# A linear-attention layer and a gated MLP in one kernel: the written order of the first part set anew

## The chip, the cores and the metric

One core of a Trainium2 chip runs the whole program. The time is the device time of one execution in microseconds (us); lower is better.

## The reference

Four sequences of 768 tokens with 8 heads of 48 channels go through a recurrent attention, and the 3072 resulting tokens of 384 channels through a gated MLP with 1536 hidden channels. All is in float32.

```python
# attention, for each batch and head, over t = 0 .. 767
cur   = outer(u * k[t], v[t])
y[t]  = r[t] @ (state + cur)
state = w[:, None] * state + outer(k[t], v[t])

# MLP on x = y, tokens by channels
gate = 1 / (1 + exp(-(x @ w_gate)))
out  = (gate * (x @ w_val)) @ w_out
```

## The kernel before, in words

**Attention.** The sequence is cut into 12 chunks of 64 steps, and the heads into two groups of four. `GROUPS` numbers the 24 pairs of chunk and head group: groups 0 and 1 are chunk 0, groups 2 and 3 are chunk 1, and so on. For a group, two input tiles come in: `chan` (queries and keys with channels on the partitions, step `L`, line 104) and `toks` (keys and values with tokens on the partitions, step `X`, line 109); each has three buffers. Of them are made, by powers of `w` in tables, scaled queries (`R`, line 309), keys (`k`, 320), keys with the bonus `u` (`A`, 296, which must read the keys before `k` writes over them), and token keys (`T`, 324). TensorE forms the scores (`Z`, line 392, 32 small matmuls, two instructions each of matmul and weight load), VectorE keeps the wanted half of them (`K`, 400), TensorE applies them to the values (`I`, 354; from chunk 1 on it adds the part from the state first, with a drain of TensorE between), and forms the outer products for the next state (`O`, 354). The result goes to the MLP's input as a rounded high part (`h`, 493, ScalarE) and a low part (`l`, 497, VectorE); the state is decayed (`d`, 447) and added to or, in chunk 0, copied (`s` on VectorE, `sa` on ScalarE, 468). Six or so small transfers fill spare rows of that input (`F`, line 501).

**MLP.** The MLP runs over tiles of 512 tokens (two chunks). The 1536 hidden channels are 12 weight blocks `f`. A product of float32 quality is made of three products of high and low parts. For a block, `u` and `v` (line 531) are nine matmuls each, gate and value; `g` (544, ScalarE), `m` (548, VectorE), `H` (553, ScalarE) and `q` or `qv` (557, GpSimd or VectorE) make the hidden values, and `D` (573) adds their product with the third weight matrix into three accumulators. The first tile takes blocks 0 and 1 in two halves of 256 columns, `a` (chunk 0) and `b` (chunk 1), because chunk 1 isn't there yet.

**Weights.** Each block is loaded once (`W`, line 242, 1152 KB; block 0 in two halves) and turned into high and low parts that stay: `c` (249, ScalarE), `j` (256, VectorE), `w` (264, ScalarE), and `o` or `ov` (267, GpSimd or VectorE). `c0`, `j0`, `w0`, `o0` with an index are the halves of block 0.

**The order.** No scheduler chooses the order: `manual_schedule` takes the instructions of all engines as they are written. The string `START` is the order of the first part. Each word is one step, and the word's place sets the place of its instructions in the queue of its engine. An engine runs its own queue in order and waits, by semaphores, for what others must have made. `N.5` is five idle matmuls on a spare tile (line 641), whose result nobody reads. After the string, a loop in the code runs the remaining tiles.

```python
    for step in START.split():
        name, _, arg = step.partition(".")
        if name == "D":
            finish(block(arg))
        elif name in moe_steps:
            moe_steps[name](moe_of(block(arg)), block(arg)[2])
        else:
            steps[name](*([int(arg)] if arg else []))
```

Matmul results of attention and of `u` and `v` share three PSUM banks (`ring`); a step that needs a bank waits for the readers of what stood there.

Of the kernel before, what the change touches and what calls it, by code (L numbers as in the profile page):

```python
# [40 lines left out]


START = """
ta L.0 tov.0 tc tb W.0 ts.0 L.1 ts.1 X.0 tz W.1 tk L.2 X.1 to.1 ti.1 X.2 ti.0 A.0 R.0 W.2 k.0 c0.0
tp tr Z.0 tt A.1 K.0 c0.1 tn k.1 I.0 Rv.1 j0.1 h.0 l.0 Tv.0 Z.1 c.1 j0.0 O.0 A.2 j.1 w0.0 sa.0 N.5
T.2 K.1 F.0 w.1 W.3 Rv.2 I.1 T.1 N.4 k.2 L.3 o0v.0 h.1 L.4 Z.2 w0.1 W.4 O.1 X.3 l.1 o0.1 s.1 u.0a
g.0a K.2 v.0a o.1 m.0a c.2 I.2 O.2 R.3 d.2 j.2 u.1a A.3 N.3 H.0a g.1a k.3 h.2 q.0a s.2 v.1a w.2 l.2
m.1a Z.3 T.3 A.4 H.1a N.4 R.4 K.3 c.3 k.4 I.3 O.3 F.2 L.5 W.8 o.2 D.0a X.4 h.3 L.6 Z.4 W.5 l.3 d.3
W.6 L.7 s.3 X.5 u.0b X.6 g.0b j.3 v.0b c.4 w.3 u.2 j.4 qv.1a m.0b H.0b g.2 v.2 q.0b K.4 w.4 Rv.5
u.1b T.4 A.5 v.1b g.1b m.1b D.0b k.5 H.1b I.4 ov.3 O.4 m.2 A.6 R.6 q.1b Z.5 k.6 L.8 d.4 D.1a W.7 h.4  # L50
o.4 s.4 H.2 D.1b K.5 c.6 l.4 Tv.5 u.3 c.5 g.3 j.6 v.3 j.5 qv.2 I.5 h.5 Z.6 l.5 R.7 L.9 A.7 m.3 X.8
d.5 D.2 ub K.6 H.3 O.5 k.7 s.5 w.5 q.3 u.4 c.8 T.6 ov.5 c.7 g.4 v.4 j.7 w.6 m.4 u.5 ov.6 g.5 v.5 I.6
Y.8 R.8 Z.7 W.9 d.6 O.6 W.10 X.7 w.7 W.11 H.4 s.6 X.9 D.3 j.8 h.6 qv.4 w.8 l.6 D.4 m.5 H.5 F.6 ov.7
qv.5 u.6 c.9 g.6 K.7 v.6 ov.8 m.6 Tv.7 H.6 u.7 qv.6 g.7 k.8 v.7 j.9 m.7 w.9 D.5 o.9 u.8 g.8 H.7 v.8
q.7 c.10 D.6 j.10 m.8 I.7 H.8 Z.8 O.7 d.7 R.9 h.7 w.10 s.7 D.7 b.8 ov.10 u.9 l.7 qv.8 g.9 c.11 v.9
F.7 Y.9 j.11 m.9 D.8 w.11 ov.11 u.10 g.10 H.9 qv.9 v.10 m.10 H.10 u.11 qv.10 g.11 t.8 i.8 v.11 K.8
k.9 m.11 D.9 H.11 t.9 D.10 q.11 b.9 T.9 i.9 T.8
"""


# [869 lines left out]
```

## Time and profile before

| | |
|---|---|
| time, median of 3 runs | 528.82 us (526.42 to 529.17) |
| the profiled execution | 528.38 us, its span 526.6 us |
| TensorE busy | 509.7 us (97%) |
| VectorE, ScalarE, GpSimd busy | 202.6, 186.1, 187.2 us (38, 35, 36%) |
| data moved by DMA | 47.84 MB, mean 91 GB/s |
| mean granted clock of TensorE | 0.995 |

The span goes from the first to the last instruction of the profiled execution; its own time has 1.8 us more around it. PE is TensorE's matmuls, PEld its weight loads, which overlap them; DVE is VectorE, ACT ScalarE, POOL GpSimd, SP the engine that issues the transfers. The granted clock is a share of 2.4 GHz: 0.50 is 1.2 GHz. "issue" as the cause of a wait means that the profile shows nothing that the engine waited for. No clock is on record before 16.46 us, and the table shows 1.00 there.

### The profile page before, as it was taken

The page shows a single profiled execution, that of the slowest core. Times are in us where ns is not written, and L with a number is a line of the kernel's source. Part 1 is how long each engine was busy: PE and PEld are TensorE (multiplying, and loading weights), DVE is VectorE, ACT ScalarE, POOL GpSimd, SP SyncE. Part 2 cuts the span into 40 slices and gives each one's busy share as a digit, 9 for nine tenths or more (in the row PEclk, how much of TensorE's full clock was granted, in tenths as well). Part 3 has the DMA queues.
Part 4 walks back from the last instruction along what each step waited for, and adds up shares of the span by engine and source line. Part 5 has one row for each costly group of instructions (what it writes and reads, how often), then busy time and mean ns, then how long its engine had stood idle before and what let it go on. Part 6 is the DMA issues. An engine that isn't in the chain of part 4 may idle for free.

```text
span 526.6 us, 11976 instructions
## 1 busy us (share of the span) xinstructions
PE 509.7 (97%) x5220; PEld 421.4 (80%) x5220; DVE 202.6 (38%) x345; ACT 186.1 (35%) x395; POOL 187.2 (36%) x158
## 2 busy tenths in 40 slices
PE   3899999999999999999999999999999999999995
PEld 3689788888888788888888888888888888888884
DVE  7877865545242243242341432431442211111112
ACT  5587864534223134233133332331431221311211
POOL 4454402214545252453452452552352111111120
PEclk9899999999999999999999999999999999999999
DMA  8949654123213030420230420312400000100001
GB/s 318 368 144 421 262 191 167 34 75 96 76 64 88 10 107 4 145 88 19 78 98 12 148 87 1 97 36 72 147 17 2 11 7 14 61 0 1 0 2 65
DMA packets 15579, 47.84 MB, mean 91 GB/s; under 512 B 2368, under 2 KB 4928, under 8 KB 14112
## 3 DMA queue, kind: packets, MB, share of 16 engines
q1 hardware_dynamic: 15376, 46.74, 25.5%
q8 instruction: 43, 0.70, 0.6%
q10 hardware_dynamic: 144, 0.26, 0.1%
...
## 4 chain that ended last, share of the span: by engine, by line
PE 95%; DVE 2%; DMA 1%; issue 1%; ACT 0%; SPq 0%; DVEq 0%; ACTq 0%
PE ring L531 56%; PE acc L573 29%; PE ring L354 7%; PE sc L392 3%; DMA chan<-in_ch 1%; DVE score L400 1%; DVE wf L256 0%; PE acc L641 0%; DVE chan L320 0%; ACT dec L296 0%; DVE sg L586 0%; DVE dec L309 0%; DVE xt L497 0%; DVE toks L324 0%; PE acc L354 0%
## 5 line engine op out<-in xcount | busy, mean ns | idle before, releaser
L531 PE MATMUL ring<-xt,wx 128*128 128x512 f32 (+1 forms) x1332 | 306.5, 384 | 0.0
L531 PEld LDWEIGHTS ring<-xt,wx 128*128 128x128 f32 x1332 | 245.2, 188 | 49.8 <-ACT sg L544 0.3
L557 POOL TENSOR_TENSOR h<-sg,h 128x512 fp32r<-128x512 f32 (+1 forms) x65 | 87.1, 1340 | 252.4 <-ACT h L553 252.4
L573 PE MATMUL acc<-h,wx 128*128 128x512 f32 (+1 forms) x666 | 161.3, 387 | 0.0
L573 PEld LDWEIGHTS acc<-h,wx 128*128 128x128 f32 x666 | 121.2, 188 | 25.0 <-DVE h L557 0.2
L548 DVE TENSOR_TENSOR sg<-ring,sg 128x512 f32<-128x512 f32 (+1 forms) x74 | 50.0, 676 | 235.0 <-PE ring L531 233.5
L544 ACT ACTIVATE sg<-ring 128x512 f32<-128x512 f32 (+1 forms) x74 | 43.2, 584 | 156.3 <-PE ring L531 156.3
L553 ACT CAST h<-sg 128x512 fp32r<-128x512 f32 (+1 forms) x74 | 45.0, 609 | 144.1 <-DVE sg L548 137.8
L309 POOL TENSOR_TENSOR dec<-chan,tabk 128x512 f32<-128x512 f32 x21 | 27.7, 1319 | 14.3 <-PE ring L354 14.0
L497 DVE TENSOR_TENSOR xt<-ring,xt 112x256 fp32r<-112x256 f32 (+1 forms) x52 | 19.9, 418 | 32.6 <-ACT xt L493 32.6
L324 POOL TENSOR_TENSOR toks<-toks,tabn 128x384 f32<-128x384 f32 x19 | 23.7, 1253 | 12.5 <-ACT wx L264 9.5
L330 POOL TENSOR_TENSOR dec<-dec,toks 128x384 f32<-128x384 f32 x16 | 16.3, 1017 | 26.9 <-DMA dec<-in_rt 26.7
L320 DVE TENSOR_TENSOR chan<-chan,tabk 128x512 f32<-128x512 f32 x24 | 24.8, 1034 | 0.6 <-ACT dec L296 0.6
L392 PE MATMUL sc<-dec,chan 48*64 48x64 f32 x768 | 17.2, 231 | 7.7 <-DVE chan L320 7.6
L400 DVE COPY_PREDICATED score<-masks,sc 128x512 f32<-128x512 int32 x32 | 23.9, 748 | 1.9 <-PE sc L392 1.1
L447 ACT ACTIVATE state<-state,pw 112x96 f32<-112x96 f32 x80 | 23.4, 362 | 1.8 <-PE ring L354 1.8
L392 PEld LDWEIGHTS sc<-dec,chan 48*64 48x64 f32 x768 | 14.8, 145 | 8.9 <-POOL dec L309 7.6
L466 DVE TENSOR_TENSOR state<-state,ring 48x192 f32<-48x192 f32 (+1 forms) x52 | 17.9, 350 | 8.1 <-PE ring L354 4.3
L256 DVE SCALAR_TENSOR_TENSOR wf<-wr,top 128x1152 int32<-128x1152 int32 (+1 forms) x13 | 16.8, 1304 | 9.5 <-ACT top L249 6.0
L354 PE MATMUL ring<-score,toks 64*48 64x64 f32 (+1 forms) x768 | 16.6, 223 | 3.7 <-issue 2.3
L493 ACT CAST xt<-ring 112x256 fp32r<-112x256 f32 (+1 forms) x52 | 16.7, 363 | 6.6 <-PE ring L354 6.4
L267 POOL TENSOR_TENSOR wx<-wf,wx 128x1152 fp32r<-128x1152 f32 (+1 forms) x5 | 12.5, 2507 | 18.3 <-ACT wx L264 18.3
...
## 6 DMA issues: line engine op xcount, KB each, us to landing
...
```

The costliest lines, as they stand in the source:

```text
L309: eng.tensor_tensor(v4(t[:, 0]), v4(chan[n][:, 0]), bc2(table_of(n)[:, :, ::-1]), ALU.mult)
L320: eng.tensor_tensor(v4(k), v4(k), bc2(table_of(n)), ALU.mult)
L324: eng.tensor_tensor(v4(k), v4(k), bc2(tabn[:, 4 * g : 4 * g + 4]), ALU.mult)
L354: nc.tensor.matmul(to[bank][64 * half : 64 * half + m, cs], lhsT, rhs, start=first, stop=stop, skip_group_check=True,)
L392: nc.tensor.matmul(sc[64 * gm : 64 * gm + 64, be, o : o + C], kk[row, cs : cs + C], rr[row, cs : cs + C], start=True, stop=True,)
L400: nc.vector.copy_predicated(t.rearrange("q (b m i) -> q b m i", b=2, m=4), masks[:, m].bitcast(I32).unsqueeze(1).unsqueeze(1).broadcast_to ...
L531: nc.tensor.matmul(o[:, self.cols], w[a][:, g * DM + kt * P : g * DM + (kt + 1) * P], self.x[:, kt, b, self.cols], start=(k == 0), stop=(k ...
L544: nc.scalar.activation(sg[:, c], self.pair[f][0][:, c], AF.Sigmoid, scale=UP)
L548: nc.vector.tensor_tensor(sg[:, c], self.pair.pop(f)[1][:, c], sg[:, c], ALU.mult)
L553: nc.scalar.copy(out=h[:, 0, c], in_=sg[:, c])
L557: eng.tensor_tensor(h[:, 1, c], self.sg.pop(f)[:, c], h[:, 0, c], ALU.subtract)
L573: nc.tensor.matmul(self.acc[d][:, self.cols], w[a][:, 2 * DM + d * P : 2 * DM + (d + 1) * P], h[:, b, self.cols], start=(f == 0 and k == 0 ...
```

## The change

Only the string `START` differs. The same steps are written in another order, some on another engine: five of the sixteen idle matmuls go (`N.5 N.4 N.3 N.4` becomes `N.5 N.4 N.1 N.1`), the first `to` (clearing a tile) goes from VectorE to GpSimd, `tr` becomes `trA` (VectorE to ScalarE), `sa.0` and `s.1` become `s.0` and `sa.1`, and some `R`, `T`, `o` and `q` change between GpSimd and VectorE. From `m.8 I.7 H.8` on, the two strings are the same again.

```diff
--- before.py
+++ after.py
@@ -41,20 +41,20 @@
 
 
 START = """
-ta L.0 tov.0 tc tb W.0 ts.0 L.1 ts.1 X.0 tz W.1 tk L.2 X.1 to.1 ti.1 X.2 ti.0 A.0 R.0 W.2 k.0 c0.0
-tp tr Z.0 tt A.1 K.0 c0.1 tn k.1 I.0 Rv.1 j0.1 h.0 l.0 Tv.0 Z.1 c.1 j0.0 O.0 A.2 j.1 w0.0 sa.0 N.5
-T.2 K.1 F.0 w.1 W.3 Rv.2 I.1 T.1 N.4 k.2 L.3 o0v.0 h.1 L.4 Z.2 w0.1 W.4 O.1 X.3 l.1 o0.1 s.1 u.0a
-g.0a K.2 v.0a o.1 m.0a c.2 I.2 O.2 R.3 d.2 j.2 u.1a A.3 N.3 H.0a g.1a k.3 h.2 q.0a s.2 v.1a w.2 l.2
-m.1a Z.3 T.3 A.4 H.1a N.4 R.4 K.3 c.3 k.4 I.3 O.3 F.2 L.5 W.8 o.2 D.0a X.4 h.3 L.6 Z.4 W.5 l.3 d.3
-W.6 L.7 s.3 X.5 u.0b X.6 g.0b j.3 v.0b c.4 w.3 u.2 j.4 qv.1a m.0b H.0b g.2 v.2 q.0b K.4 w.4 Rv.5
-u.1b T.4 A.5 v.1b g.1b m.1b D.0b k.5 H.1b I.4 ov.3 O.4 m.2 A.6 R.6 q.1b Z.5 k.6 L.8 d.4 D.1a W.7 h.4
-o.4 s.4 H.2 D.1b K.5 c.6 l.4 Tv.5 u.3 c.5 g.3 j.6 v.3 j.5 qv.2 I.5 h.5 Z.6 l.5 R.7 L.9 A.7 m.3 X.8
-d.5 D.2 ub K.6 H.3 O.5 k.7 s.5 w.5 q.3 u.4 c.8 T.6 ov.5 c.7 g.4 v.4 j.7 w.6 m.4 u.5 ov.6 g.5 v.5 I.6
-Y.8 R.8 Z.7 W.9 d.6 O.6 W.10 X.7 w.7 W.11 H.4 s.6 X.9 D.3 j.8 h.6 qv.4 w.8 l.6 D.4 m.5 H.5 F.6 ov.7
-qv.5 u.6 c.9 g.6 K.7 v.6 ov.8 m.6 Tv.7 H.6 u.7 qv.6 g.7 k.8 v.7 j.9 m.7 w.9 D.5 o.9 u.8 g.8 H.7 v.8
-q.7 c.10 D.6 j.10 m.8 I.7 H.8 Z.8 O.7 d.7 R.9 h.7 w.10 s.7 D.7 b.8 ov.10 u.9 l.7 qv.8 g.9 c.11 v.9
-F.7 Y.9 j.11 m.9 D.8 w.11 ov.11 u.10 g.10 H.9 qv.9 v.10 m.10 H.10 u.11 qv.10 g.11 t.8 i.8 v.11 K.8
-k.9 m.11 D.9 H.11 t.9 D.10 q.11 b.9 T.9 i.9 T.8
+ta tk L.0 to.0 tz X.1 tc A.0 ti.1 tb tp k.0 X.0 ti.0 to.1 L.1 R.0 trA W.0 Z.0 tt ts.0 c0.0 Rv.1 A.1
+tn L.2 K.0 k.1 I.0 h.0 ts.1 W.1 j0.0 l.0 w0.0 c0.1 R.2 Tv.0 L.3 A.2 X.2 Z.1 O.0 K.1 c.1 j0.1 N.5 s.0
+I.1 N.4 w0.1 T.1 o0.0 L.4 h.1 k.2 Z.2 j.1 O.1 l.1 K.2 R.3 F.0 I.2 Tv.2 W.2 u.0a o0.1 X.3 w.1 o.1 T.3
+A.3 k.3 d.2 O.2 N.1 X.5 g.0a T.5 h.2 A.4 v.0a N.1 W.3 sa.1 s.2 l.2 Z.3 F.2 c.2 u.1a m.0a K.3 k.4
+H.0a q.0a g.1a j.2 L.5 I.3 h.3 W.5 v.1a l.3 d.3 m.1a D.0a R.4 Z.4 O.3 u.0b s.3 c.3 W.4 u.1b w.2 v.0b
+g.0b ov.2 H.1a j.3 w.3 A.5 q.1a u.2 m.0b H.0b g.2 qv.0b v.2 g.1b W.6 c.5 m.2 j.5 D.0b o.3 u.3 L.6
+K.4 H.2 c.4 v.1b X.4 q.2 v.3 X.7 g.3 D.1a j.4 m.1b L.8 Rv.5 c.6 k.5 Tv.4 I.4 W.7 Z.5 O.4 w.5 m.3
+Tv.7 d.4 A.6 X.6 h.4 ov.5 R.6 w.4 k.6 s.4 K.5 ov.4 D.2 u.5 H.3 W.8 W.11 H.1b l.4 q.3 j.6 g.5 T.6 D.3
+qv.1b u.4 g.4 v.5 D.1b w.6 v.4 c.8 L.7 m.5 ub c.7 m.4 H.4 qv.4 W.10 o.6 j.8 u.6 I.5 d.5 Z.6 O.5 h.5
+g.6 A.7 D.4 j.7 s.5 K.6 l.5 H.5 v.6 R.7 I.6 w.7 W.9 o.7 q.5 k.7 c.9 Z.7 O.6 X.8 d.6 m.6 w.8 j.9 o.8
+u.7 h.6 c.10 H.6 D.5 g.7 l.6 s.6 v.7 u.8 v.8 qv.6 m.7 D.6 F.6 Y.8 w.9 L.9 R.8 X.9 H.7 k.8 j.10 K.7
+ov.9 g.8 qv.7 m.8 I.7 H.8 Z.8 O.7 d.7 R.9 h.7 w.10 s.7 D.7 b.8 ov.10 u.9 l.7 qv.8 g.9 c.11 v.9 F.7
+Y.9 j.11 m.9 D.8 w.11 ov.11 u.10 g.10 H.9 qv.9 v.10 m.10 H.10 u.11 qv.10 g.11 t.8 i.8 v.11 K.8 k.9
+m.11 D.9 H.11 t.9 D.10 q.11 b.9 T.9 i.9 T.8
 """
 
 
```

**TensorE, around block 1.** In these rows L531 on 128x256 is `u` or `v` of a half block, L641 an idle matmul and its weight load, L392 the scores of one group (here Z.3, the fourth group), and `ring<-dec,state` the part of `I` that comes from the state. Before, from the last idle matmul ahead of `v.1a` on:

```order
L641 LDWEIGHTS spare
L641 MATMUL acc_540<-spare 128x512
L531 MATMUL ring<-xt,wx 128x256 x9
L392 MATMUL sc<-dec,chan 64x64 x16
L392 MATMUL sc<-chan,dec 64x64 x16
L641 LDWEIGHTS spare
L641 MATMUL acc_610<-spare 128x512
```

And now, from the idle matmul ahead of `v.0a` on:

```order
L641 MATMUL acc_510<-spare 128x512
L531 MATMUL ring<-xt,wx 128x256 x9
L641 LDWEIGHTS spare
L641 MATMUL acc_534<-spare 128x512
L392 MATMUL sc<-dec,chan 64x64 x16
L392 MATMUL sc<-chan,dec 64x64 x16
L531 MATMUL ring<-xt,wx 128x256 x9
L354 MATMUL ring<-dec,state 64x64 x2
L354 MATMUL ring<-dec,state 48x64 x2
```

Z.3 stands ahead of block 1 now (the first row with L531 is `v.0a`, the second `u.1a`), and `I.3` begins right behind `u.1a`, before `v.1a`. Single idle matmuls stand where three and four stood.

**VectorE, from the first group's low part on.** L497 is `l`, L324 `T`, L256 the joins `j`, L400 the masks `K` (`score_98` is `K.1`, `score_97` `K.2`), L468 state copies, L320 keys. Before:

```order
L497 TENSOR_TENSOR xt<-ring,xt 112x2x128 x2
L324 TENSOR_TENSOR toks<-toks,tabn 128x384
L256 SCALAR_TENSOR_TENSOR wf<-wr,top_120 128x576
L256 SCALAR_TENSOR_TENSOR wf<-wr,top_121 128x1152
L400 COPY_PREDICATED score_98<-masks,sc 128x512 x2
L309 TENSOR_TENSOR dec<-chan,tabk 128x512
L320 TENSOR_TENSOR chan<-chan,tabk 128x512
L267 TENSOR_TENSOR wx<-wf,wx 128x576
L497 TENSOR_TENSOR xt<-ring,xt 48x2x128 x4
L468 COPY state<-acc_410 112x2x96
L468 COPY state<-acc_411 112x2x96
L400 COPY_PREDICATED score_97<-masks,sc 128x512 x2
```

And now:

```order
L497 TENSOR_TENSOR xt<-ring,xt 112x2x128 x2
L324 TENSOR_TENSOR toks<-toks,tabn 128x384
L400 COPY_PREDICATED score_98<-masks,sc 128x512 x2
L256 SCALAR_TENSOR_TENSOR wf<-wr,top_120 128x576
L468 COPY state<-ring 112x2x96 x2
L320 TENSOR_TENSOR chan<-chan,tabk 128x512
L256 SCALAR_TENSOR_TENSOR wf<-wr,top_121 128x1152
L497 TENSOR_TENSOR xt<-ring,xt 48x2x128 x4
L400 COPY_PREDICATED score_97<-masks,sc 128x512 x2
L324 TENSOR_TENSOR toks<-toks,tabn 128x384
```

`K.1` stands ahead of the joins of the second half of block 0 and of block 1 now. The state copy is that of group 0 out of `ring`; before it was that of group 1 out of an accumulator, behind `l.1`. `K.2` follows `l.1` directly.

**SP, the first transfers.** Buffers have numbers here. `chan` and `toks` are the input tiles of a group, 128x2304 is half of weight block 0, 128x4608 a whole block, and `xt` the row fills. Before:

```order
L242 DMA wr_138<-in_wt 128x2304 x2
L104 DMA chan_142<-in_ch 128x1024
L109 DMA toks_145<-in_tk 128x800
L242 DMA wr_148<-in_wt 128x4608
L104 DMA chan_158<-in_ch 128x1024
L109 DMA toks_160<-in_tk 128x800
L109 DMA toks_164<-in_tk 128x800
L242 DMA wr_173<-in_wt 128x4608
L501 DMA xt_252<-xt_252 16x2x256 x6
L242 DMA wr_337<-in_wt 128x4608
L104 DMA chan_365<-in_ch 128x1024
```

And now:

```order
L104 DMA chan_134<-in_ch 128x1024
L109 DMA toks_138<-in_tk 128x800
L109 DMA toks_158<-in_tk 128x800
L104 DMA chan_162<-in_ch 128x1024
L242 DMA wr_169<-in_wt 128x2304 x2
L104 DMA chan_219<-in_ch 128x1024
L242 DMA wr_246<-in_wt 128x4608
L104 DMA chan_258<-in_ch 128x1024
L109 DMA toks_264<-in_tk 128x800
L104 DMA chan_353<-in_ch 128x1024
L501 DMA xt_242<-xt_242 16x2x256 x6
L242 DMA wr_463<-in_wt 128x4608
```

Two token tiles and the second group's channels (`chan_162`) stand ahead of block 0 now. The fourth group's channels (`chan_258`) stand behind block 1 and ahead of block 2 (`wr_463`), and the row fills of the first chunk ahead of block 2. The fourth group's tokens follow behind block 2.

## Rows read from the trace of the kernel before

**Rows 1.** the page: busy time by engine, and fetches of instructions (packets, MB, share)
```profile
PE 509.7 (97%) x5220; PEld 421.4 (80%) x5220; DVE 202.6 (38%) x345; ACT 186.1 (35%) x395; POOL 187.2 (36%) x158
...
q8 instruction: 43, 0.70, 0.6%
```

**Rows 2.** table of stretches: busy us and count by engine, clock, DMA share, GB/s
```profile
7.62:16.46 8.84, 8.10 (x199) 6.59 (x200) 8.27 (x16) 6.21 (x16) 0.00 (x0) 1.00 1.03 426
...
19.88:23.29 3.41, 3.41 (x66) 1.99 (x64) 2.02 (x5) 2.14 (x5) 0.98 (x1) 0.50 0.89 352
...
37.92:126.60 88.68, 88.02 (x1099) 73.87 (x1094) 58.53 (x86) 52.14 (x100) 28.30 (x21) 1.00 0.46 174
```

**Rows 3.** timeline of TensorE's matmuls: start, us, line, operation, count, idle time before
```profile
7.62 1.13 PE L392 MATMUL sc<-dec,chan 48*64 48x64 f32 x32 [7.62 <-DVE chan L320]
...
12.51 1.14 PE L392 MATMUL sc<-dec,chan 48*64 48x64 f32 x32
...
14.26 1.09 PE L354 MATMUL ring<-toks 64*64 64x48 f32 x32
...
17.63 0.56 PE L354 MATMUL ring<-score,toks 64*64 64x64 f32 x20 [0.53 <-DVE score L400]
19.56 0.43 PE L354 MATMUL ring<-score,toks 64*48 64x64 f32 x12 [1.37 <-issue]
...
21.74 1.14 PE L392 MATMUL sc<-dec,chan 48*64 48x64 f32 x32
...
23.96 2.51 PE L531 MATMUL ring<-xt,wx 128*128 128x256 f32 x18
26.40 0.68 PE L354 MATMUL ring<-dec,state 48*64 48x64 f32 x32
27.37 0.68 PE L354 MATMUL ring<-score,toks 64*64 64x64 f32 x32 [0.29 <-issue]
...
32.61 1.04 PE L641 MATMUL acc<-spare 128*128 128x512 bf16 x4
33.58 0.68 PE L354 MATMUL ring<-dec,state 48*64 48x64 f32 x32
...
37.92 7.36 PE L531 MATMUL ring<-xt,wx 128*128 128x256 f32 x42
```

**Rows 4.** timeline of ScalarE
```profile
5.32 1.28 ACT L296 ACTIVATE dec<-chan,wu 128x128 f32<-128x128 f32 x4 [3.07 <-DMA chan<-in_ch]
...
39.75 1.53 ACT L249 ACTIVATE top<-wr 128x1152 f16<-128x1152 bf16 x1
```

**Rows 5.** table of stretches around the order's first difference
```profile
0.00:18.60 18.60, 9.31 (x221) 7.15 (x222) 15.92 (x31) 11.27 (x24) 8.14 (x19) 1.00 0.89 345
18.60:23.96 5.36, 4.40 (x112) 2.88 (x111) 3.30 (x6) 2.14 (x5) 2.04 (x3) 0.68 0.89 307
23.96:26.40 2.44, 2.44 (x23) 2.26 (x19) 2.15 (x4) 1.07 (x2) 2.39 (x1) 1.00 1.04 399
```

**Rows 6.** timeline of VectorE
```profile
20.80 1.73 DVE L497 TENSOR_TENSOR xt<-ring,xt 48x256 fp32r<-48x256 f32 x4 [0.59 <-ACT xt L493]
24.11 0.62 DVE L468 COPY state<-acc 112x192 f32<-112x192 f32 x2 [1.58 <-PE acc L354]
24.75 1.56 DVE L400 COPY_PREDICATED score<-masks,sc 128x512 f32<-128x512 int32 x2
...
27.21 1.89 DVE L256 SCALAR_TENSOR_TENSOR wf<-wr,top 128x1152 int32<-128x1152 int32 x1 [0.21 <-ACT top L249]
...
38.78 1.35 DVE L256 SCALAR_TENSOR_TENSOR wf<-wr,top 128x1152 int32<-128x1152 int32 x1
```

**Rows 7.** timeline of SP's queue, the row fills of the third group
```profile
31.84 4.58 SPq L501 DMA_DIRECT2D xt<-xt  x6
```

**Rows 8.** instruction fetches between 16.8 and 18.1 us (packets, MB, share)
```profile
q8 instruction: 1, 0.02, 5.1%
```

**Rows 9.** instruction fetches between 23.2 and 24.3 us
```profile
q8 instruction: 1, 0.02, 5.2%
```

## Prediction

> **What bounds the kernel now.** I read the page first, then the table of stretches, then the timelines of the engines in the first 40 us. On the page TensorE is busy for 509.7 of 526.6 us, and no other engine comes above 38% [rows 1]. The table says where the rest is: from 37.92 to 126.60 us TensorE lacks 0.66 us of 88.68 [rows 2]. So from 37.92 us on, TensorE's own work sets the time, and the written order can win next to nothing there; it can only lose, by bringing a weight block or a state too late. What the order can win lies ahead of 37.92 us, where block 0 begins its second half (`u.0b`). There the timeline of TensorE [rows 3] shows four kinds of loss:
>
> - the wait of 7.62 us before the first scores;
> - at 17.63 us a wait of 0.53 us, and at 19.56 us one of 1.37 us that no semaphore explains ("issue"), in the middle of `I.1`;
> - a stretch from 19.88 to 23.29 us with a granted clock of 0.50, that is 1.2 instead of 2.4 GHz [rows 2], right behind those two waits;
> - sixteen idle matmuls (`N`, line 641), of which four take from 32.61 to 33.58 us, 0.24 us each.
>
> The new order does the same real work before `u.0b`: scores Z.0 to Z.4, I and O of four groups, u and v of blocks 0 and 1 for the first half, and D.0a. So the question is when `u.0b` starts, against 37.92 us, and whether TensorE waits behind it.
>
> **Up to the first scores: nothing.** The first channels land at about 5.3 us, when ACT's `A.0` starts; it takes 1.28 us [rows 4], `k.0` follows, and Z.0 starts at 7.62 us. Both orders have this chain. The clearing that moves from VectorE to GpSimd stands ahead of `R.0` there, but two score clearings go behind it, and `R.0` has the 7.62 us as cover; were that gone, the price would be some tenths.
>
> **Second group: later by 0.3 us, covered.** In the new queue order the second channels land behind the first and two token tiles; ScalarE's `A.1`, though, now stands behind `c0.0`, which waits for the first half of block 0's weights. Four transfers ahead of it and itself are 512+400+400+512+576 KB, 2.46 MB; at about 0.43 MB/us, by the 426 GB/s of that time [rows 2], the last four are there 4.5 us after 5.3, at 9.8 us. With `c0.0` (half a block, at most 0.8 of the 1.53 us of a whole one) and 1.28 us, `A.1` ends at about 12.0 us [rows 4]; `k.1` some 0.7 us later; Z.1 starts at 12.8, not 12.51 us [rows 3]. Z.1 took 1.75 us to O.0's start, so `K.1` begins at 14.7 us. It takes some 1.5 us, then come `j0.1` (half of a 1.35 us join) and the state copies `s.0` (0.62) [rows 6], which now are VectorE's and hold a bank of `I.1`: 17.5 us. `I.1` started at 17.63 us. I take no change; earlier than 17.2 it can't be, and an idle matmul row stands in that cover.
>
> **The instruction stall: stays.** The page has 43 instruction fetches on queue 8 for 10,440 matmuls and weight loads of TensorE, about 243 for each fetch [rows 1]. By 18.6 us 443 instructions had run [rows 5], when TensorE stopped without a wait. The sequence of TensorE is the same in both orders up to O.1, so the stall stands at the same instruction. Its size depends on the transfers beside it, which are others now: from 0 to 1.6 us. I keep 1.37 us, and the half clock behind it.
>
> **From 21.74 us on, step by step.** Z.2 starts at 21.74, O.1 ends near 24.0 us [rows 3]. Here the order differs. Before: block 0 (`u.0a`, `v.0a`), `I.2`, `O.2`, block 1. After: `I.2`, `u.0a`, `O.2`, one idle matmul, `v.0a`, one more, Z.3, `u.1a`, `I.3`, `v.1a`, D.0a, Z.4, O.3, `u.0b`. `I.2` needs `K.2`, which stands behind `l.1` (ends at 22.53 us [rows 6]) and needs the last of Z.2, some 23.6 us: with 1.56 us it is done at 25.15. The state part of `I.2` fills 24.0 to 24.97 (26.40 to 27.37 in the rows), so the score part waits 0.18 us more than before.
>
> From 23.96 to 37.92 us are 13.96 us [rows 3]. Five idle matmuls of seven go: 5 x 0.23 = 1.15 us. 24.0 + 13.96 - 1.15 + 0.18 = 36.99 us: **a gain of 0.93 us**. The other inputs of these steps by their rows: `l.2` ends near 29.0 us, and its six row fills took 4.58 us to issue on SP [rows 7] and 2 to 3 us to land, near 36 us, 1 us ahead of `u.0b`. `K.3` follows Z.3 (30.3 us) and is done at 31.8, when `I.3`'s state part runs. `v.1a` needs the bank that `g.1a` frees; ScalarE has `sa.1`, `c.2` and `H.0a` ahead of that and gets there near 32.2 us, 0.6 us before `v.1a`.
>
> **Behind `u.0b`.** `u.2` follows after three products of 1.22 us, near 40.6 us. Its weights: `h.3` ends near 34.4 on ScalarE, then `d.3`, `c.3` and `w.2` follow, none longer than the 1.53 us of a cast of a whole block [rows 4]: with 1.2 us for the two shorter ones 38.3, at most 39.0 us. `ov.2` on VectorE is as large as a join, 1.35 us [rows 6]: 39.6 us, 1.0 us of slack (at the bound 0.2), the least I find. `o.3` has 1.2 us before `u.3`, `ov.5` some 2 us before `u.5`. SP stands at `X.6` until O.4 (near 55 us) with blocks 8, 11, 10 and 9 queued behind it; the first of them is wanted 20 us later. All of it fits, so the lead passes through to the end. The profiled execution took 528.38 us for its span of 526.6; 528.38 - 0.93 = **527.4 us**. That execution lies 0.44 us under the median of the runs, 528.82. The upper bound of the gain is all that TensorE loses in this stretch and the order could touch; the lower bound is below zero, by the rivals.
>
> **Rivals.**
>
> *The next instruction fetch comes too late (0.24).* The first fetch's packet lies between 16.8 and 18.1 us [rows 8], and TensorE went on at 19.56, some 1.5 us behind it. The next one lies between 23.2 and 24.3 us [rows 9], so it is usable near 25.8 us. Before, instruction 443 + 243 = 686 came between 666 (23.96 us) and 708 (26.40) [rows 5], in block 0, whose matmuls use few instructions in much time. Now it falls into `I.2`'s state part, at 24.2 us. TensorE would stand until 25.8 instead of 25.15 and still have some 0.6 us of state part left: 1.2 us lost. Time: 527.4 + 1.2 = 528.6 us. Against it: one such stall shows in the whole trace.
>
> The Trainium skill (Runtime: NRT & Kernel Launch, section Instruction fetch mechanics) says that instructions come in blocks of 16 KiB and that crossing from one to the next is mostly hidden. By that rule this rival would be nothing and the time 527.4 us; the 1.37 us in the rows speak against it where attention steps, with many short instructions, run beside full transfers.
>
> *The stall and the half clock go (0.19).* If the first fetch, beside smaller transfers, arrives in time, `I.1` ends at 18.25 us, `l.1` ends as before 2.55 us behind it (19.99 to 22.53 [rows 3, 6]), at 20.8, `K.2` at 22.4, and `I.2`'s score part runs at 22.5 instead of 25.15 us: 2.65 us more, 524.8 us. Against it: the same instruction, the same busy queues.
>
> *VectorE is late and the time ends above before (0.17).* Its operations lengthen when GpSimd works beside them: the same join took 1.89 us at 27.21 and 1.35 us at 38.78 us [rows 6]. Between 25.15 and 39.6 us the new order gives it twelve steps (`K.3`, `j.2`, `l.3` and `ov.2` the longest). If eight of them take 0.54 us more, 4.3 us in all, the 1.0 us of slack at `ov.2` is used up from the second on, and TensorE waits some 3.4 us in `I.3`, `u.2` and what follows. Time: 527.4 + 3.4 = 530.8 us. It decides from 0.93 + 1.0 us of loss on. For it: VectorE was busy for 2.15 of 2.44 us around `u.0a` [rows 5]. Against it: before, VectorE was as full, and TensorE had no such wait behind 37.92 us.
>
> **How the numbers follow.** The likeliest case, 527.4 us, gets 0.40, and the three rivals what stands beside them. Half a percent, 2.6 us, is about what a measurement of this kernel can tell from no change: the three runs of before differ by that much. From the median that is below 526.2 or above 531.4 us. Faster: most of the third case and a little of the first, 0.22. Slower: VectorE late, where it is a little worse than priced, and a late fetch that comes together with it, 0.14. The same: 0.64. The range goes from the third case, 524.7, to VectorE's, 530.9 us; what is left out is a larger gain where several losses go at once, or a wait that I haven't seen.
>
> **What would show it.** Right: `u.0b` near 37.0 us; the "issue" wait of over a microsecond in `I.1` and 0.50 clock after it; `I.2` ahead of `u.0a` with a short wait for `K.2`; no wait over 0.3 us behind `u.0b`. Wrong: a second "issue" wait near 24 us (the first rival); a clock of 1.00 from 17 us on (the second); waits for VectorE's tiles before `u.2` or `I.3` (the third). I am wrong altogether if TensorE shows idle time in blocks 2 to 11, where I expect none.

## The result and the profile after

The changed kernel takes 531.76 us (median of 7 runs, 530.99 to 533.28), the kernel before 528.91 us beside it. The ratio is 1.0055 (95% interval 1.0036 to 1.0073): the change made the kernel slower by 0.55%. Forecast were 527.4 us and a range of 524.7 to 530.9.

The profiled execution took 533.28 us for its span of 531.1, the slowest of the seven; that of before, 528.38 us, lay under its median. So the two traces differ by 4.9 us and the medians by 2.85. On the page TensorE's busy time has hardly moved [rows 1], so the time is in waits:

```profile
PE 510.2 (96%) x5215; PEld 423.0 (80%) x5215; DVE 205.3 (39%) x339; ACT 187.7 (35%) x398; POOL 196.3 (37%) x161
```

The table of TensorE's waits names what it stood for: sum, times, longest.

```profile
PE sc L392 <- POOL score L139: 8.1, 1, 8.1
PE ring L354 <- issue: 2.0, 7, 0.7
PE ring L354 <- DMA wr<-in_wt: 1.7, 1, 1.7
PE ring L531 <- POOL h L557: 1.4, 1, 1.4
PE ring L354 <- DVE xt L497: 0.9, 1, 0.9
PE acc L573 <- DVE h L557: 0.6, 1, 0.6
```

The timeline of TensorE's matmuls tells where, beside [rows 3]:

```profile
8.13 1.14 PE L392 MATMUL sc<-dec,chan 48*64 48x64 f32 x32 [8.13 <-POOL score L139]
...
19.30 0.43 PE L354 MATMUL ring<-score,toks 64*48 64x64 f32 x12 [0.27 <-issue]
...
20.62 0.69 PE L392 MATMUL sc<-dec,chan 48*64 48x64 f32 x32
...
23.22 0.66 PE L354 MATMUL ring<-dec,state 48*64 48x64 f32 x30 [0.87 <-DVE xt L497]
25.57 1.12 PE L354 MATMUL ring<-score,toks 64*64 64x64 f32 x32 [1.69 <-DMA wr<-in_wt]
26.61 2.29 PE L531 MATMUL ring<-xt,wx 128*128 128x256 f32 x9
...
33.38 1.33 PE L531 MATMUL ring<-xt,wx 128*128 128x256 f32 x9
...
40.09 5.11 PE L531 MATMUL ring<-xt,wx 128*128 128x256 f32 x34
...
48.97 0.62 PE L573 MATMUL acc<-h,wx 128*128 128x256 f32 x3 [0.56 <-DVE h L557]
...
85.73 2.34 PE L531 MATMUL ring<-xt,wx 128*128 128x512 f32 x9 [1.39 <-POOL h L557]
...
125.90 0.65 PE L392 MATMUL sc<-dec,chan 48*64 48x64 f32 x32
```

Z.0 comes 0.51 us late. The 1.37 us in I.1 has shrunk to 0.27, and Z.2 starts 1.1 us earlier than before. Then I.2 stands twice, and `u.0b` starts at 40.09 us, 2.17 late. Behind it come 0.56 us at D.0b and 1.39 at `u.7`. The sum is 4.12 us; Z.9, behind all of this, starts at 125.90 us, before at 121.77:

```profile
121.77 0.65 PE L392 MATMUL sc<-dec,chan 48*64 48x64 f32 x32
```

The second wait of I.2 is put down to a transfer, but the weight load of that matmul shows `DVE score L400`, K.2. The timeline of VectorE and GpSimd shows why K.2 is late:

```profile
18.60 1.22 DVE L320 TENSOR_TENSOR chan<-chan,tabk 128x512 f32<-128x512 f32 x1
19.24 1.84 POOL L267 TENSOR_TENSOR wx<-wf,wx 128x576 fp32r<-128x576 f32 x1
19.75 2.55 DVE L256 SCALAR_TENSOR_TENSOR wf<-wr,top 128x1152 int32<-128x1152 int32 x1
22.22 1.74 DVE L497 TENSOR_TENSOR xt<-ring,xt 48x256 fp32r<-48x256 f32 x4
...
23.99 1.52 DVE L400 COPY_PREDICATED score<-masks,sc 128x512 f32<-128x512 int32 x2
```

The join `j.1` (L256), written ahead of l.1 (L497) and K.2 (L400), takes 2.55 us beside GpSimd's o0.1, against 1.35 in [rows 6]. l.1 starts only at 22.22 us. I.2 takes two of the three banks, and its second one is free only when l.1 has read it: the wait of 0.87 us. The table of stretches shows what follows, at a granted clock of 0.50, and the rest of the first tile:

```profile
24.85:31.67 6.82, 6.10 (x81) 5.58 (x82) 3.63 (x7) 2.93 (x11) 3.37 (x3) 0.50 0.75 301
37.92:126.60 88.68, 85.92 (x1133) 72.36 (x1135) 59.02 (x82) 51.90 (x94) 33.28 (x20) 1.00 0.49 182
```

The 6.10 us of work at 1.2 GHz would take about half at 2.4 GHz: some 3 us lost, where before 3.41 us ran at half clock [rows 2]. `u.0a` alone takes 2.29 us; `u.1a`, nine such matmuls at full clock, takes 1.33 (33.38 in the timeline).

### The profile page after: what moved, and what is told of

It reads as the page before. It is cut to its first block, busy times and chain, and to the rows that moved or that the text cites. A ratio compares the mean times of both kernels' runs of the same rounds, so it can differ in the third digit from the quotient of the medians.

```text
span 531.1 us, 11963 instructions
## 1 busy us (share of the span) xinstructions
PE 510.2 (96%) x5215; PEld 423.0 (80%) x5215; DVE 205.3 (39%) x339; ACT 187.7 (35%) x398; POOL 196.3 (37%) x161
## 4 chain that ended last, share of the span: by engine, by line
PE 87%; DMA 3%; issue 2%; SPq 2%; ACT 2%; DVE 1%; POOL 1%; POOLq 0%; ACTq 0%; DVEq 0%
PE ring L531 52%; PE acc L573 28%; PE ring L354 6%; DMA wr<-in_wt 3%; PE sc L392 2%; SPq L501 1%; POOL wx L267 1%; ACT dec L296 1%; DVE wf L256 0%; ACT wx L264 0%; POOL dec L309 0%; DVE h L557 0%; SPq L104 0%; POOL h L557 0%; SPq L109 0%
## 5 line engine op out<-in xcount | busy, mean ns | idle before, releaser
L531 PE MATMUL ring<-xt,wx 128*128 128x512 f32 (+1 forms) x1332 | 308.9, 386 | 1.4 <-POOL h L557 1.4
L531 PEld LDWEIGHTS ring<-xt,wx 128*128 128x128 f32 x1332 | 246.7, 190 | 50.8 <-POOL h L557 1.5
L309 POOL TENSOR_TENSOR dec<-chan,tabk 128x512 f32<-128x512 f32 x22 | 30.2, 1375 | 20.5 <-PE ring L354 20.5
L497 DVE TENSOR_TENSOR xt<-ring,xt 112x256 fp32r<-112x256 f32 (+1 forms) x52 | 19.9, 418 | 30.5 <-ACT xt L493 30.4
L400 DVE COPY_PREDICATED score<-masks,sc 128x512 f32<-128x512 int32 x32 | 23.9, 747 | 2.3 <-PE sc L392 1.5
L392 PE MATMUL sc<-dec,chan 48*64 48x64 f32 x768 | 16.7, 227 | 8.3 <-POOL score L139 8.1
L320 DVE TENSOR_TENSOR chan<-chan,tabk 128x512 f32<-128x512 f32 x24 | 24.2, 1009 | 0.6 <-ACT dec L296 0.6
L324 POOL TENSOR_TENSOR toks<-toks,tabn 128x384 f32<-128x384 f32 x18 | 23.2, 1294 | 0.8 <-DMA toks<-in_tk 0.8
L256 DVE SCALAR_TENSOR_TENSOR wf<-wr,top 128x1152 int32<-128x1152 int32 (+1 forms) x13 | 21.0, 1625 | 5.0 <-ACT top L249 3.3
L267 POOL TENSOR_TENSOR wx<-wf,wx 128x1152 fp32r<-128x1152 f32 (+1 forms) x7 | 17.7, 2533 | 13.7 <-ACT wx L264 13.7
L392 PEld LDWEIGHTS sc<-dec,chan 48*64 48x64 f32 x768 | 14.4, 142 | 9.2 <-POOL score L139 8.1
L354 PEld LDWEIGHTS ring<-score,toks 64*48 64x48 f32 (+1 forms) x768 | 14.6, 134 | 5.5 <-issue 3.3
```

Source lines behind the costliest of these rows:

```text
L309: eng.tensor_tensor(v4(t[:, 0]), v4(chan[n][:, 0]), bc2(table_of(n)[:, :, ::-1]), ALU.mult)
L320: eng.tensor_tensor(v4(k), v4(k), bc2(table_of(n)), ALU.mult)
L354: nc.tensor.matmul(to[bank][64 * half : 64 * half + m, cs], lhsT, rhs, start=first, stop=stop, skip_group_check=True,)
L392: nc.tensor.matmul(sc[64 * gm : 64 * gm + 64, be, o : o + C], kk[row, cs : cs + C], rr[row, cs : cs + C], start=True, stop=True,)
L400: nc.vector.copy_predicated(t.rearrange("q (b m i) -> q b m i", b=2, m=4), masks[:, m].bitcast(I32).unsqueeze(1).unsqueeze(1).broadcast_to ...
L531: nc.tensor.matmul(o[:, self.cols], w[a][:, g * DM + kt * P : g * DM + (kt + 1) * P], self.x[:, kt, b, self.cols], start=(k == 0), stop=(k ...
```

## The experiments

Each ratio is to the kernel before, timed on the same chip beside it. "Boundary n" is the n-th matmul or weight load on record. The diffs show the words around an edit, not whole lines of the string.

### The wait at u.7

The edit, on the changed kernel, is to GpSimd's and ScalarE's order.

```diff
-w.3 A.5 q.1a u.2 m.0b H.0b g.2 qv.0b
+w.3 q.1a u.2 m.0b H.0b A.5 g.2 qv.0b
-w.7 W.9 o.7 q.5 k.7
+w.7 W.9 q.5 o.7 k.7
```

> The changed kernel with q.5 ahead of o.7 on GpSimd, and H.0b ahead of A.5 on ScalarE. Theory A (u.7 waits 1.39 us through q.5 on GpSimd, D.0b 0.56 us for qv.0b behind H.0b): both waits go, time 1.5 to 2 us less, 529.8 to 530.3. Rival (u.7 waits for o.7 itself, whose end the trace shows too early): o.7 ends 0 to 1.3 us later and the wait stays or grows to 2.7 us, time 531.2 to 532.5.

Measured: 532.22 us, ratio 1.0058 (1.0037 to 1.0079). Both waits stayed. At `u.7` the same 1.39 us, now without a releaser, though q.5 was done long before:

```profile
84.26 2.35 PE L531 MATMUL ring<-xt,wx 128*128 128x512 f32 x9 [1.39 <-issue]
```

My theory on q.5 fell. The rival fell too, since o.7 ended at 83.04 us. At D.0b 0.38 us stayed; why is told in the last section.

What it was came out of the next two kernels, made for the first part (below). Both stood near `u.7` as well; the one with seven idle matmuls more ahead stood inside O.6. The place in the program had moved and the number of the instruction had not. This table, from the tables of stretches, the timelines and the fetch windows, holds all runs that stood there:

| run | records before the stop | where | stood, us | fetch starts | goes on |
|---|---|---|---|---|---|
| changed kernel | 2720 | u.7 | 1.39 | 83.4 | 85.73 |
| join later | 2720 | u.7 | 1.77 | 81.2 | 83.55 |
| seven idle matmuls | 2722 | in O.6 | 1.80 | 81.1 | 83.82 |
| q.5 first | 2720 | u.7 | 1.39 | 82.0 | 84.26 |
| clearing later | 2720 | u.7 | 1.75 | 83.3 | 86.28 |
| I.2 back | 2721 | u.7 | 1.50 | 84.0 | 86.68 |
| before, shifted by 80 | 2721 | in O.6 | 1.79 | 76.0 | 78.69 |

Each time a 16 KB fetch on queue 8 began 2.3 to 3.0 us ahead of the restart. For the changed kernel, the stretch up to the stop (1360 matmuls and 1360 weight loads) and the fetch between 83.3 and 83.5 us:

```profile
0.00:85.72 85.72, 70.97 (x1360) 59.90 (x1360) 63.88 (x92) 57.10 (x117) 41.24 (x39) 0.96 0.71 272
...
q8 instruction: 1, 0.02, 31.3%
```

So the theory now was a late instruction fetch. Two kernels tested it. One gives it time, on the changed kernel:

```diff
-w.7 W.9 o.7 q.5 k.7 c.9 Z.7 O.6
+w.7 W.9 q.5 o.7 k.7 c.9 Z.7 D.5 O.6
-H.6 D.5 g.7
+H.6 g.7
```

> The changed kernel with q.5 ahead of o.7 on GpSimd and D.5 (nine matmuls of 512 columns, over 2 us) moved between Z.7 and O.6. Theory F: the 1.4 to 1.8 us in which TensorE stood at u.7 in four runs of the changed order is a late instruction fetch; it stood each time at about the 2721st matmul or weight load, also where seven idle matmuls ahead of it shifted the program (there it fell into O.6). With D.5 between the request (some 100 instructions earlier) and that instruction, the fetch has 2 us more: the stall goes, or stays under 0.4 us, and the time is 530.0 to 530.5 against 531.7. Rival: u.7 waits for GpSimd's low part o.7 of its weights: o.7 ends up to 1.3 us later here, the wait stays 1.3 us or more, in D.5 or u.7, time 531.5 or above.

Measured: 530.90 us, ratio 1.0026 (1.0006 to 1.0046). In the timeline of TensorE the stop is gone, with o.7 ending as late as 83.27 us:

```profile
82.56 2.33 PE L573 MATMUL acc<-h,wx 128*128 128x512 f32 x9
84.83 0.67 PE L354 MATMUL ring<-toks 64*64 64x48 f32 x32
85.43 4.83 PE L531 MATMUL ring<-xt,wx 128*128 128x512 f32 x20
```

The other makes such a stop in the kernel before, where there was none, by shifting the program:

```diff
-H.1a N.4 R.4
+H.1a N.4 n.40 R.4
+            nc.tensor.matmul(t[0:64, 0:64], bits[:, 0:64], bits[:, 0:64], start=True, stop=True)
```

> The kernel before with 40 small idle matmuls (64x64, 80 instructions with their weight loads) behind N.4, which shifts what comes later by 80 instructions; they take 1.0 to 1.5 us themselves. Theory F: the boundary near instruction 2721, which in the kernel before lies some 60 instructions behind O.6, in long matmuls, falls into O.6 now, in the dense run of I.6, Z.7 and O.6: a stall of 1.0 to 1.8 us without a releaser there, near 76 us, where the kernel before has none; time 531.0 to 532.0 (1.2 for the matmuls and 1.4 for the stall). Rival (no such boundary): no wait over 0.3 us behind u.0b, time 529.8 to 530.4.

Measured: 535.99 us, ratio 1.0142 (1.0098 to 1.0185), more than expected. The timeline of TensorE has the stop in O.6, nine matmuls ahead of its end, and a second one that I had not foreseen, at boundary 1959, with 3.41 us of half clock behind it:

```profile
53.86 0.99 PE L573 MATMUL acc<-h,wx 128*128 128x256 f32 x7 [2.36 <-issue]
...
76.39 0.52 PE L354 MATMUL ring<-toks 64*48 64x48 f32 x23
78.69 0.32 PE L354 MATMUL ring<-toks 64*48 64x48 f32 x9 [1.79 <-issue]
```

The boundaries on record, 443, 697, 948, 1959 and 2720, lie 253 apart on average. In the changed order I.6, Z.7 and O.6 (320 instructions in 3 us) end just at 2720. In the order of before they end some 60 instructions ahead of it, in front of long matmuls.

The Trainium skill (Runtime: NRT & Kernel Launch, section Instruction fetch mechanics) has blocks of 256 instructions, and the spacing here agrees. It also calls a crossing mostly hidden; by these runs that holds behind long matmuls. Inside or just behind runs of short ones TensorE stood 1.17 to 2.36 us at most of the boundaries looked at here, and 0.73 us or less where the fetch had begun early or another wait had covered part of it.

### Ahead of u.0b

The join behind l.1 and K.2, on the changed kernel:

```diff
-k.2 Z.2 j.1 O.1 l.1 K.2 R.3
+k.2 Z.2 O.1 l.1 K.2 j.1 R.3
```

> The changed kernel with j.1 (the join of block 1) behind l.1 and K.2. Theory A (VectorE reaches l.1 and K.2 late because the join stands ahead of them; I.2 waits 0.87 and 1.69 us for them; the half clock of 6.83 us follows from those waits): l.1 starts near 20.4, K.2 is done near 23.7 instead of 25.5 us, I.2 waits under 0.8 us in all, the half clock goes or shortens, u.0b starts at 35.5 to 38.0 instead of 40.09 us; time 527 to 530 against 531.8 for the changed kernel. Theory B (the loss sits behind u.0b, and what is won ahead of it is lost again in later waits): u.0b earlier, time still above 531. Theory C (the join is then late for block 1): a wait of 1 to 2 us at u.1a in place of the one at I.2, time within 0.5 us of 531.8.

Measured: 531.63 us, ratio 1.0059 (1.0036 to 1.0081). l.1 started at 20.11 and K.2 was done at 23.37 us, as theory A said, and `u.0b` came at 38.33. But in I.2's state part a fetch took the place of the bank, at boundary 697, and half the clock loss stayed (3.41 us at 0.50):

```profile
23.34 0.45 PE L354 MATMUL ring<-dec,state 48*48 48x64 f32 x17 [1.28 <-issue]
...
83.55 2.34 PE L531 MATMUL ring<-xt,wx 128*128 128x512 f32 x9 [1.77 <-issue]
```

Idle matmuls in the time of the wait, on the changed kernel:

```diff
-R.3 F.0 I.2
+R.3 F.0 N.7 I.2
```

> The changed kernel with seven idle matmuls between O.1 and I.2, in time in which TensorE stood (1.6 of 2.56 us). K.2 stays where it is, so the score part of I.2 still starts near 25.6 us. Theory A (the clock falls because TensorE stood there): granted clock 1.00 through block 0, u.0a and what follows at the full-clock durations, u.0b near 37.3 us, time near 529. Rival (the clock falls for another reason, or falls anyway at the short waits left): half clock for 6.8 us again, u.0b near 40 us, time 531.5 to 532.

Measured: 531.65 us, ratio 1.0042 (1.0020 to 1.0064). The clock stayed at 1.00 through block 0, `u.0a` took 1.33 us and `u.0b` started at 38.10, as theory A said. It is not this execution alone: the mean granted clock was 0.997 or more in 9 of its 12, and in 2 of 7 of the changed kernel. Yet stops of 1.0 to 1.5 us alone don't bring the half clock each time; three runs below had them and kept 1.00 there. In the profiled execution the 2 us were lost in block 7, where the fetch stop was followed by a half clock that the changed kernel's trace does not have there:

```profile
83.82 0.31 PE L354 MATMUL ring<-toks 64*64 64x48 f32 x6 [1.80 <-issue]
84.06 3.71 PE L531 MATMUL ring<-xt,wx 128*128 128x512 f32 x9
```

The start: GpSimd's second clearing later.

```diff
-ti.0 to.1 L.1 R.0 trA W.0 Z.0 tt ts.0 c0.0
+ti.0 L.1 R.0 trA W.0 Z.0 tt ts.0 to.1 c0.0
```

> The changed kernel with the second clearing of a top tile (to.1) behind R.0 and the score clearing on GpSimd. Theory: VectorE's two token powers took 1.84 instead of 0.87 us beside it, so k.0 and Z.0 came 0.5 us late; here Z.0 starts at 7.6 to 7.8 instead of 8.13 us, and the lead lasts: time 531.2 to 531.4. Rival: Z.0 comes earlier, but I.1 and I.2 wait as much longer for VectorE, u.0b as in the changed kernel's runs (38.8 to 40.1), time 531.5 to 532.

Measured: 532.61 us, ratio 1.0060 (1.0036 to 1.0085). Z.0 came at 7.97 us, 0.16 earlier, and VectorE's two token powers still took 1.77 us. My theory was wrong: the powers (`tp`) now stand ahead of `k.0` on VectorE. Before, its timeline had them behind:

```profile
6.62 0.90 DVE L320 TENSOR_TENSOR chan<-chan,tabk 128x512 f32<-128x512 f32 x1 [0.33 <-ACT dec L296]
7.44 0.87 DVE L169 TENSOR_TENSOR pw<-pw 128x256 f32<-128x256 f32 x2
```

That `k.0` first would give the 0.5 us back is read from these rows and was not tried.

The repairs known by then together: join later, clearing later, H.0b ahead of A.5, D.5 ahead of O.6 (the diffs above).

> The changed kernel with j.1 behind K.2, to.1 behind the score clearing, H.0b ahead of A.5, q.5 ahead of o.7 and D.5 between Z.7 and O.6: all losses found so far at once. If they add up: 0.5 at Z.0, 0.5 to 1.7 in I.2 and the half clock, 0.4 to 0.56 at D.0b, 1.4 to 1.8 at u.7, 2.8 to 4.5 us in all, time 527.2 to 528.9, at or under the kernel before. Rival (VectorE and the fetches give waits elsewhere): 529.5 to 531.

Measured: 530.58 us, ratio 1.0026 (1.0009 to 1.0043): the rival. `u.0b` at 38.41 us, without a half clock ahead of it; the fetch at 697 cost 1.53 us, and `v.0a` waited 1.37 us for g.0a, which stands on ScalarE behind w.1 and so behind the join.

I.2 back behind block 0, on the changed kernel, where only what depends on it moves along:

```diff
-l.1 K.2 R.3 F.0 I.2 Tv.2 W.2 u.0a o0.1 X.3 w.1 o.1 T.3
-A.3 k.3 d.2 O.2 N.1 X.5 g.0a T.5 h.2 A.4 v.0a N.1 W.3
+l.1 K.2 R.3 F.0 Tv.2 W.2 u.0a o0.1 X.3 w.1 o.1 T.3
+A.3 k.3 g.0a v.0a m.0a N.1 I.2 d.2 O.2 X.5 T.5 h.2 A.4 N.1 W.3
```

> The changed kernel with I.2 back behind block 0 (u.0a, v.0a, one idle matmul, I.2), where it stood before; nothing else but m.0a, d.2 and g.0a, which must go along. Theory A (the part of the change that hurts ahead of u.0b is I.2 next to O.1, where it waits for its bank behind l.1, for K.2, and for the fetch near instruction 697): u.0a waits for l.1 alone, up to 2.0 us, I.2 has no wait over 0.4, u.0b starts at 37.0 to 38.3 against 38.8 to 40.3 us in the runs of the changed order; the fetch wait of 1.4 to 1.8 us at u.7 stays; time 530.0 to 531.0 against 531.8. Rival (l.1 is late whatever follows it): the wait only moves to u.0a, with the half clock behind it, u.0b from 38.8 us on, time 531.5 or above.

Measured: 532.14 us, ratio 1.0060 (1.0039 to 1.0081), `u.0b` at 41.70 us: the rival.

> Both repairs: I.2 back behind block 0, and D.5 between Z.7 and O.6 with q.5 ahead of o.7. If the two losses are independent: the one of the run with I.2 back, less 1.4 to 1.8 us for the fetch at u.7: 528.3 to 529.4, level with the kernel before. Rival (what is won early is lost later): 530 or above.

Measured, with the D.5 repair: 529.75 us, ratio 1.0025 (1.0004 to 1.0046), `u.0b` at 38.20 us. So the D.5 repair is worth the same here, but I.2's place is worth nothing. `u.0a` waited 1.02 and 1.40 us for l.1, I.2 had no wait over 0.29, and O.2 and Z.3, now back to back, met the boundary at 948. In the timeline of the second:

```profile
23.76 2.17 PE L531 MATMUL ring<-xt,wx 128*128 128x256 f32 x16 [1.02 <-DVE xt L497]
...
30.23 0.28 PE L392 MATMUL sc<-dec,chan 48*64 48x64 f32 x4 [1.17 <-issue]
```

In the first it was 2.13 us there, and 6.83 us of half clock behind it.

Next, with the D.5 repair and H.0b ahead of A.5, l.1 ahead of the join as well, and w.1 and o.1 behind g.0a:

```diff
-k.2 Z.2 j.1 O.1 l.1 K.2 R.3 F.0 I.2
+k.2 Z.2 O.1 l.1 F.0 K.2 j.1 R.3
-u.0a o0.1 X.3 w.1 o.1 T.3
+u.0a o0.1 X.3 T.3 g.0a v.0a w.1 o.1 A.3 k.3 m.0a N.1 I.2
```

> Both repairs, and VectorE's l.1 and K.2 ahead of the join j.1, with w.1 and o.1 behind g.0a, H.0b ahead of A.5. Theory: l.1 is done near 22.0 us, u.0a starts there without a wait over 0.6, the boundary near instruction 697 falls behind 2.5 us of long matmuls and costs at most 0.4, no half clock; u.0b at 35.0 to 36.8 us; time 526.0 to 528.0, under the kernel before. Rival (the join and what follows it are now late for block 1): a wait of 1 to 2.5 us at u.1a, time 528.5 to 530.

Measured: 532.92 us, ratio 1.0060 (1.0036 to 1.0085). Block 0 and I.2 ran without a wait from 22.58 us, as expected. Neither the theory nor the rival foresaw the rest: Z.3 stood for k.3, behind the moved join, and for the fetch, and 10.24 us of half clock followed:

```profile
29.24 0.62 PE L392 MATMUL sc<-dec,chan 48*64 48x64 f32 x25 [1.38 <-DVE chan L320]
30.37 0.38 PE L392 MATMUL sc<-dec,chan 48*64 48x64 f32 x4 [0.51 <-issue]
...
30.08:40.32 10.24, 9.67 (x130) 8.96 (x130) 7.40 (x11) 6.79 (x17) 5.00 (x4) 0.50 0.43 142
```

Last, the run with both repairs and block 1's long matmuls ahead of Z.3:

```diff
-h.2 A.4 N.1 W.3 sa.1 s.2 l.2 Z.3 F.2 c.2 u.1a K.3 k.4
-H.0a q.0a g.1a j.2 L.5 I.3 h.3 W.5 v.1a l.3 d.3 m.1a D.0a
+h.2 A.4 u.1a N.1 W.3 sa.1 s.2 l.2 v.1a Z.3 F.2 g.1a c.2 K.3 k.4
+H.0a q.0a j.2 L.5 I.3 h.3 W.5 m.1a l.3 d.3 D.0a
```

> The run with both repairs, and u.1a and v.1a moved ahead of Z.3, so that three dense steps (I.2, O.2, Z.3) no longer follow one another. In the two runs with I.2 behind block 0, TensorE stood 1.17 and 2.13 us in Z.3 at the 949th instruction, 506 behind 443 and 1772 ahead of 2721: a fetch boundary of the same kind, every 253 instructions. Theory F: with 2.5 us of long matmuls ahead of Z.3 that wait is at most 0.4 us; u.0b starts at 37.0 to 37.7 instead of 38.20 us; time 528.7 to 529.4. Rival (v.1a now waits for the bank behind l.2 on VectorE, 0.5 to 1.5 us, or a half clock follows from it): time 529.7 or above.

Measured: 530.11 us, ratio 1.0022 (1.0004 to 1.0041). The stop in Z.3 is gone, as theory F said, and VectorE's K.3 and l.2 take its place at I.3 and O.3 (1.16, 0.62 and 0.58 us); `u.0b` at 38.83 us:

```profile
30.91 0.69 PE L392 MATMUL sc<-dec,chan 48*64 48x64 f32 x32
...
33.70 0.68 PE L354 MATMUL ring<-score,toks 64*64 64x64 f32 x32 [1.16 <-DVE score L400]
...
38.24 0.66 PE L354 MATMUL ring<-toks 64*64 64x48 f32 x30 [0.58 <-DVE xt L497]
```

### The first part or the rest

Here the string of one kernel up to `u.0b` is joined to the string of the other behind it.

> The order of before up to u.0b, the changed order behind it, there with D.5 between Z.7 and O.6 and q.5 ahead of o.7. Theory (what the two repairs left, some 0.25%, is lost ahead of u.0b, in VectorE's late l.1 and K.2 and the waits that follow): with the old first part only the 0.3 to 0.6 us at D.0b are left; ratio to the kernel before 0.999 to 1.002, time 528.6 to 529.8. Rival (it is lost behind u.0b, where the changed order keeps more of GpSimd beside VectorE): ratio 1.002 to 1.004, time 530 to 531.

> The changed order up to u.0b, the order of before behind it (with ov.2, w.2 and what else of block 2 the changed order does there placed ahead of u.0b). Theory: the early loss stays, u.0b from 38.7 to 40.3 us, no fetch wait at u.7, since the dense steps stand further apart there: ratio 1.002 to 1.005, time 530 to 531.5. Rival: 0.999 to 1.002, 528.6 to 529.8.

> As the run with the old first part, with five fewer idle matmuls in it (N.3 and N.4 become N.1 and N.1). If these are on TensorE's path: u.0b up to 1.15 us earlier, time 527.7 to 528.8. Rival (waits for VectorE's K.3 and l.1 take their place, as in the run of the kernel before with the same five left out): within 0.5 us of the run with the old first part.

Measured: 535.58, 537.65 and 533.98 us, ratios 1.0106, 1.0143 and 1.0097. These three settle nothing: where the halves meet, weights come in the wrong order. In the first, ScalarE's c.5 waited 6.96 us for its block, which stood behind block 8 in SP's queue, and TensorE stood 3.55 and 0.80 us at I.4; in the second, c.4 waited 4.19 us for block 4, queued behind block 5. So the queue of the first and third was set right:

```diff
-F.2 L.5 W.8 o.2 D.0a X.4 h.3 L.6 Z.4 W.5 l.3 d.3 W.6 L.7 s.3 X.5 u.0b
+F.2 L.5 o.2 D.0a h.3 Z.4 W.5 l.3 d.3 W.6 s.3 X.5 u.0b
```

> The old first part with the changed rest again, now without the seam that spoilt the first attempt: in the queue of transfers W.8, X.4, L.6 and L.7 stand behind W.5 and W.6, where the changed rest has them (in the first attempt block 5's weights came behind block 8's, and TensorE stood 4.35 us at I.4). Theory (what the repair at u.7 leaves is lost ahead of u.0b): u.0b 37.3 to 38.0, waits behind it of 0.6 us or less, Z.9 within 0.7 us of the kernel before, ratio 0.998 to 1.002. Rival (it is lost behind u.0b): waits of 1 us or more there, ratio 1.002 to 1.004.

Measured: 528.25 us, ratio 0.9997 (0.9976 to 1.0018): the theory. `u.0b` at 36.44 us, Z.9 at 120.47, no wait over 0.29 us between them (lines are one lower in this file):

```profile
36.44 5.90 PE L530 MATMUL ring<-xt,wx 128*128 128x256 f32 x37
...
120.47 0.65 PE L391 MATMUL sc<-dec,chan 48*64 48x64 f32 x32
```

From `u.0b` to Z.9 these are 84.03 us, in the kernel before 83.85 and in the changed kernel 85.81. The changed rest, with D.5 repaired, costs nothing that the interval would show.

### The idle matmuls

The predicted gain was five idle matmuls. Left out of the kernel before, and of the last run:

```diff
-u.1a A.3 N.3 H.0a
+u.1a A.3 N.1 H.0a
-H.1a N.4 R.4
+H.1a N.1 R.4
```

> The kernel before with three plus two fewer idle matmuls (N.3 and N.4 become N.1 and N.1 at the same places). The prediction's term: five at 0.23 us, u.0b 1.15 us earlier at 36.8 us, time 527.8 against 528.9. Rival (they stood in waits that come back): u.0b within 0.3 us of 37.92 and time within 0.3 us of 528.9. Second rival (they kept the clock up): a stretch of half clock between 28 and 38 us, time 529.5 to 532.

Measured: 528.64 us, ratio 0.9989 (0.9966 to 1.0012).

> The same with five fewer idle matmuls (N.3, N.4 become N.1, N.1). If they are on TensorE's path: 0.5 to 1.15 us less than the run without this; ratio 0.996 to 1.000. Rival: the waits for VectorE (l.1, K.3) take their place, within 0.3 us of it.

Measured: 529.07 us, ratio 1.0004 (0.9986 to 1.0021). `u.0b` started at 36.37 and 36.41 us, against 36.44 with all of them. That is in part chance: in both, I.1, which stands ahead of the idle matmuls left out, waited longer for its mask (0.84 and 1.44 us), and block 0 came later. From the start of I.2 to `u.0b` it took 11.36 us in both, 11.52 in the kernel before, and 12.30 in the run with all of them, where O.3 stood 0.49 us for GpSimd's token keys. Against the kernel before 0.16 us is left of the 1.15: `v.1a` follows `u.1a` after 1.81 us as before, now waiting 0.24 us for ScalarE's g.1a, and I.3 waits 0.71 us for its mask. These are the rows of the second run (lines one lower again), and the last is I.3 in the kernel before:

```profile
28.89 1.33 PE L530 MATMUL ring<-xt,wx 128*128 128x256 f32 x9 [0.24 <-ACT sg L543]
...
32.95 0.68 PE L353 MATMUL ring<-score,toks 64*64 64x64 f32 x32 [0.71 <-DVE score L399]
...
34.50 0.68 PE L354 MATMUL ring<-score,toks 64*64 64x64 f32 x32 [0.24 <-DVE score L400]
```

## Why the prediction was wrong

The sum of the loss: with the stop at `u.7`, six of the changed orders lie at 1.0042 to 1.0060; four without it at 1.0022 to 1.0026 (a fifth, with 10.24 us of half clock, at 1.0060). The D.5 repair is worth about 0.3%, 1.6 us. The rest, some 0.25% or 1.3 us, is lost ahead of `u.0b`, since the old first part brings the ratio to 0.9997. The intervals of single runs overlap; it is the four at 1.0022 to 1.0026 agreeing that bears this out.

- **"Behind u.0b: all of it fits, so the lead passes through to the end"** is the step that failed. I checked there that data would come in time, weights and states, and not that instructions would. TensorE's queue had no late operand at `u.7`; its program was late, by 1.39 us. At D.0b an operand was late after all, by 0.56 us: VectorE's qv.0b, held up beside GpSimd (last section).
- **The first rival**, a late fetch, had the mechanism and the price (1.2 us; measured 1.28 to 1.53 in I.2's state part). It put the boundary at instruction 686, the runs at 697. In the changed kernel the wait for the bank covered it. I looked for one more boundary, and the same arithmetic, carried on by 253, gives the one at `u.7`.
- **"From 21.74 us on, step by step"**: K.2's end was nearly right (25.15 forecast, 25.51 measured), but by accident. Z.2 came 1.1 us early and VectorE was late by as much. I.2's state part was taken as gapless, though it needs a bank that l.1 must free (0.87 us), and no price was put on a half clock behind the waits, some 3 us in the profiled execution.
- **The 1.15 us for five idle matmuls** measured nothing in the time, and 0.16 us in the traces: most of them stood in waits for ScalarE and VectorE that come back.
- **"The instruction stall: stays"** failed the other way. In six other traces with the old first part, I.1 stood at most 0.29 us at boundary 443 five times and 0.73 us once. The fetch began between 14.8 and 16.1 us in those five, at 16.8 in the sixth, and at 16.9 in the profile of before. Its 1.37 us belong to that execution, and the half clock behind them comes in some executions only, as told below; I had built on both as if fixed.
- **"Up to the first scores: nothing"**: 0.5 us, since `tp` passed `k.0` on VectorE, as far as the rows say. I had read GpSimd's order there and not VectorE's.
- **VectorE late**, the third rival, had the right engine and cause, at the join ahead of l.1 and not at `ov.2`.

What stays open: how the 1.3 us ahead of `u.0b` divide between VectorE, the fetches and the clock. Each repair there moved the wait to the next of the three. The mean granted clock of each execution narrows it for the clock. In the 19 traces it is 0.996 or less where 3.41 us or more ran at half clock ahead of the kernel's end, and 0.997 or more where none did. By that sign 43 of the 133 executions of the kernel before that were timed beside the experiments had such a stretch (median 530.2 us, against 528.6 for the other 90), and 5 of 7 of the changed kernel. Its other two took 530.99 and 531.58 us, so most of the 2.85 us is not the half clock. No version measured beats the kernel before.
